# Four transposes of a head pair's outputs, spread between the products with V

## The chip, the cores and the metric

The kernel runs on one core of a Trainium2 chip. The metric is the device time of one execution in microseconds (us). Three runs of the kernel before gave 708.21, 708.3 and 709.0 us, so the median is 708.3 us.

## The reference

One transformer block with adaptive layer norm: 2048 tokens, model width 448, 16 heads of width 28, a sliding window of 256 keys, and a Mish feed-forward of width 1792.

```python
x = A_x
mod = (_silu(c) @ w_mod).reshape(c.shape[0], 6, 1, -1)
sa, ca, ga, sb, cb, gb = (mod[:, 0], mod[:, 1], mod[:, 2], mod[:, 3], mod[:, 4], mod[:, 5])
h = _layernorm(x, axis=-1) * (1 + ca) + sa
x = x + ga * _A_ref(h, A_wqkv, A_wo)       # softmax(mask(q k^T / sqrt(28))) v, then @ wo
h = _layernorm(x, axis=-1) * (1 + cb) + sb
x = x + gb * _B_ref(h, B_w1, B_b1, B_w2)   # mish(h @ w1 + b1) @ w2
```

All of it is float32. The mask keeps key k for query q where 0 <= q - k < 256.

## The kernel before

The 2048 tokens are cut into NG = 4 groups of GT = 512. For each group the kernel makes the normalized input, transposes it (`gen_hT`), and computes queries, keys and values (`gen_qkv`). Each float32 factor is split into a high and a low part, typed fp32r, and a product is made of the pairs high-high, high-low and low-high, so that one tile takes 11 matmuls.

Attention works on "slots". A slot i is one head of one group, and there are NS = 64 slots. Each slot has three units, so there are NU = 192 units u = 3i + b. A unit is one PSUM bank of scores: `B(u)` multiplies keys by queries (tile `sB`), adds the mask by bf16 products with an identity, and lets ScalarE write the exponentials twice (`P` in f32, `Ph` in fp32r). `SP(u)` lets GpSimd write the low part `Pl` = P - Ph. `PV(u, Ph)` and `PV(u, Pl)` multiply the two parts by V and add them up in the bank `pv` of the slot. V carries a column of ones, so that a row of `pv` is the softmax denominator. `A(i, t)` (tile `sA`) and `M2` find the row maxima that the scores are shifted by.

The units of a slot differ in shape. Unit b = 1 has two blocks of 256 columns in groups 1 to 3, and one block of 256 columns in group 0. The other two have blocks of 128 and 384 columns (group 0: one of 384, and both). A block is one matmul with V as its weights (60 columns).

When all three units of a slot are done, `EV(i)` copies `pv` into half of a tile `O2`: slots 2p and 2p+1 form head pair p (31 of the 32 pairs are touched by the change). `E(p)` transposes this tile by TensorE, in four steps of 128 tokens (124 rows, tile `et`, bank `tr`). `E2(p)` on ScalarE copies the low-part columns out (`ol`), and `E3(p)` on VectorE and GpSimd adds the parts, divides by the denominator and writes the result (`on`).

The order is written out by hand in one loop over u. Each engine runs its own instructions in program order. In step u = 3s + k the kernel writes, in this order: pending output steps, `PV(u-3, Pl)`, `EV`, `B(u)`, `SP(u-1)`, `A`, `M2`, loads, `E`/`E2`/`E3`, pieces of the next group's projections ("fillers"), a second `A`, and `PV(u-2, Ph)`. So the products of unit v with Ph end step v+2, and those with Pl begin step v+3: on TensorE they stand side by side. `E(p)` stands in step 6p+11, `E2(p)` in 6p+12 and `E3(p)` in 6p+13. The bank `tr` has one buffer, which `E` shares with `M2`.

Lines that the text speaks of: L679 `A`, L687 `M2`, L709 and L720 `B`, L723 and L724 its exponentials, L731 `SP`, L741 `PV`, L755 `E`, L760 `E2`, L768 to L771 `E3`, L250 transposes of a group's input (`tr`), L262 their low part (`hl`), L315 projection products, L595 an f32 product with a matrix of ones (`gb`), which is not split.

Of the kernel before, what the change touches and what calls it, by code (L numbers as in the profile page):

```python
# [14 lines left out]
S, D, F, H, DH, W = 2048, 448, 1792, 16, 28, 256  # L15
# [36 lines left out]
def adaln_block(ctx: ExitStack, tc: tile.TileContext, x, wqkv, wo, w1, b1, w2, c, w_mod, out):  # L52
    nc = tc.nc
    PE, ACT, DVE, POOL = nc.tensor, nc.scalar, nc.vector, nc.gpsimd
# [37 lines left out]
    def bank(tag, bufs, name):  # L92
        return PS[0].tile([128, 512], F32, name=name, tag=tag, bufs=bufs)
# [18 lines left out]
    for k in range(4):  # L112
        wmf = st0.tile([128, 2 * D], F32, name=f"wm01_{k}")
        t = wmf[0:112]
# [11 lines left out]
    for part in range(3):  # L126
        for ci in range(4):
            r0, r1 = ci * 128, min(ci * 128 + 128, D)
            for h in ((slice(0, 128),) if ci < 3 else (slice(0, 64), slice(64, 128))):
                t = wqs[ci][h]  # L130
# [9 lines left out]
    ident = cst.tile([128, 128], F32, name="ident")  # L140
# [164 lines left out]
    def drain(*gs):  # L305
        for g in gs:
            for _ in g:
                pipe.step()
# [17 lines left out]
    def flush():  # L326
        while later:
            later.pop(0)()
# [69 lines left out]
    for t in range(4):  # L398
        ln_stats(xs0[t][:, 0:D], mv0[:, t, :], qk, f"a0{t}")
        if t % 2:  # L400
            h = slice(t - 1, t + 1)
# [117 lines left out]
    O2 = []  # L519
    for i in range(2):  # L520
        t = att.tile([128, GT], F32, name=f"o2_{i}")
# [146 lines left out]
    NS = NG * H  # L668
    mx, Pt, Ph, Pl, pvb, et, olt = {}, {}, {}, {}, {}, {}, {}
    junk = att.tile([128, 384], F32, name="junk")  # L670

    def A(i, t):
        g, h = divmod(i, H)
        q, k = Q3[i % NQ], K3[i % NK]
        if i % 2 == 0 and t == 0:
            mx[i // 2] = att.tile([128, 2, 4], F32, name=f"mx{i}", tag="mx", bufs=2)
        c0 = max(256 - 128 * t, 0) if g == 0 else 0
        p = bank("sA", 2, f"sA{i}_{t}")
        PE.matmul(p[:, c0:384], q[0:84, t * 128:(t + 1) * 128], k[0:84, t * 128 + c0:t * 128 + 384],  # L679
                  start=True, stop=True)  # L680
        DVE.tensor_tensor_reduce(out=junk[:, c0:384], in0=p[:, c0:384], in1=mask[:, c0:384], scale=1.0,  # L681
                                 scalar=-3.0e38, op0=ALU.add, op1=ALU.max,
                                 accum_out=mx[i // 2][:, i % 2, t:t + 1])
# [11 lines left out]
    def units(g, b):  # L695
        return [x for x in BLOCKS[b] if g > 0 or x[0] >= 2]

    def by_width(blocks):
        return sorted(blocks, key=lambda x: x[2] - x[1])

    def B(u):
        i, b = divmod(u, 3)
        g, h = divmod(i, H)
        q, k = Q3[i % NQ], K3[i % NK]
        bl = units(g, b)
        c0 = bl[0][3]
        p = bank("sB", 2, f"sB{u}")
        for n, (jj, t0, t1, c) in enumerate(by_width(bl)[::-1]):
            PE.matmul(p[:, c:c + 128 * (t1 - t0)], k[:, jj * 128:(jj + 1) * 128], q[:, t0 * 128:t1 * 128],  # L709
                      start=(n == 0), stop=False, skip_group_check=True)  # L710
        far = {c + 128 * (jj - t0) for jj, t0, t1, c in bl if t0 <= jj < t1}
        diag = {c + 128 * (jj - 2 - t0) for jj, t0, t1, c in bl if t0 <= jj - 2 < t1}
        masked = []
        for c in sorted(far | diag):
            if c in far:
                masked.append((256 if c + 128 in diag else 128, c, 0))
            elif c - 128 not in far:
                masked.append((128, c, 128))
        for n, c, m in sorted(masked):
            PE.matmul(p[:, c:c + n], identr, fdmask[:, m:m + n], start=False, stop=True, skip_group_check=True)  # L720
        P = Pt[u] = att.tile([128, 512], F32, name=f"P{u}", tag="P", bufs=3)
        Ph[u] = att.tile([128, 512], F32R, name=f"Ph{u}", tag="Ph", bufs=3)
        ACT.activation(P[:, c0:], p[:, c0:], AF.Exp, scale=SCALE)  # L723
        ACT.activation(Ph[u][:, c0:], p[:, c0:], AF.Exp, scale=SCALE)  # L724

    def SP(u):
        i, b = divmod(u, 3)
        c0 = units(i // H, b)[0][3]
        Pl[u] = att.tile([128, 512], F32R, name=f"Pl{u}", tag="Pl", bufs=3)
        for eng, a, b in ((POOL, c0, 512),) if u < NU - 5 else ((POOL, 0, 256), (DVE, 256, 512)):  # L730
            eng.tensor_tensor(Pl[u][:, a:b], Pt[u][:, a:b], Ph[u][:, a:b].bitcast(F32), op=ALU.subtract)  # L731

    def PV(u, P):
        i, b = divmod(u, 3)
        g, h = divmod(i, H)
        if P is Ph and b == 0:
            pvb[i] = bank("sA", 2, f"pv{i}") if NS - 3 <= i < NS - 1 else bank("pv", 1, f"pv{i}")
        pv = pvb[i]
        for n, (jj, t0, t1, c) in enumerate(by_width(units(g, b))):
            j = 4 * g - 2 + jj  # L740
            PE.matmul(pv[0:60, t0 * 128:t1 * 128], V[j % NV][:, h, :], P[u][:, c:c + 128 * (t1 - t0)],  # L741
                      start=(P is Ph and b == 0 and n == 0), stop=False, skip_group_check=True)

    def EV(i):
        o = O2[i // 2 % 2][64 * (i % 2):64 * (i % 2) + 60]
        if i < NS - 3:
            ACT.activation(o, pvb[i][0:60, :], AF.Copy)  # L747
        else:
            DVE.tensor_copy(o, pvb[i][0:60, :])

    def E(pr):
        g, h = divmod(2 * pr, H)
        p = bank("tr", 1, f"et{pr}")
        for t in range(4):
            PE.transpose(p[:, t * 128:t * 128 + 124], O2[pr % 2][0:124, t * 128:(t + 1) * 128], ident[0:124, 0:124])  # L755
        et[pr] = p.rearrange("p (t a d) -> p t a d", t=4, a=2)

    def E2(pr):
        olt[pr] = att.tile([128, 4, 2, 28], F32, name=f"ol{pr}", tag="ol", bufs=2)
        ACT.activation(olt[pr], et[pr][:, :, :, 32:60], AF.Copy)  # L760

    def E3(pr):
        g, h = divmod(2 * pr, H)
        e, ol = et[pr], olt[pr]
        if h == 0:
            on[g] = mid.tile([128, 4, 512], F32, name=f"on{g}", tag="on")
        rc = att.tile([128, 4, 2, 1], F32, name=f"rc{pr}", tag="rc", bufs=2)
        DVE.reciprocal(rc, e[:, :, :, 28:29])  # L768
        DVE.tensor_tensor(ol, ol, e[:, :, :, 0:28], op=ALU.add)
        o = on[g][:, :, h * DH:(h + 2) * DH].rearrange("p t (a d) -> p t a d", a=2)  # L770
        POOL.tensor_tensor(o, ol, rc.to_broadcast([128, 4, 2, 28]), op=ALU.mult)  # L771
        if h == H - 2:
            POOL.tensor_copy(on[g][:, :, D:512], on[g][:, :, 384:448])
            on_full.add(g)
# [210 lines left out]
    def step(g):  # L985
        return next(fillers[g], 99.0) or RATE[g]
# [40 lines left out]
    for u in range(NU + 9):  # L1027
        s, k = divmod(u, 3)
        g = s // H
        if k == 0 and s % H == 0 and 0 < g < NG:  # L1030
            drain(fillers[g - 1], side[g - 1])
            flush()
        pipe.step()
        if 0 <= u - 3 < NU:
            PV(u - 3, Pl)
            if (u - 3) % 3 == 2:
                EV((u - 3) // 3)
        if u < NU:
            B(u)
        if 0 <= u - 1 < NU:  # L1040
            SP(u - 1)
        a = s + LEAD
        if a < NS:
            A(a, (0, 1, 3)[k])
        if k == 0 and (a - 1) % 2 == 1 and LEAD <= a - 1 < NS:
            M2((a - 1) // 2)
        if k == s % 2 and s < NS:
            load_slot(s + LEAD + 2)
        if s % 2 == 1 and 1 <= (s - 1) // 2 <= NS // 2:
            pr = (s - 3) // 2  # L1050
            if k == 2 and pr >= 0:
                E(pr)
        if s % 2 == 0 and k < 2 and 0 <= (s - 4) // 2 < NS // 2:
            (E2, E3)[k]((s - 4) // 2)
        if g < NG:
            v = u - 48 * g
            if v in (0, 12):
                chunk["v"] = 4 if v == 0 and g or 0 < g < NG - 1 else 2
            if v == 0:
                credit = 0.0  # L1060
            credit += RATE[g] * (2 if v < FRONT[g] else 1)
            while credit > 0.0:
                credit -= step(g)
            if v > 1 or g == 0:
                side_step(g, ("dve", "act")[a >= NS:] if k == 1 else ("act",) if k == 0 and s % 2 == 0 else ())
            if later and ((s + (k == 2)) % 2 == 0 or k == 1):
                later.pop(0)()
        if u == NU:
            drain(fillers[NG - 1], side[NG - 1])
            while pipe.items:  # L1070
                pipe.step()
            flush()
        if u - NU in TAIL:
            TAIL[u - NU]()
        if k == 1 and a < NS:
            A(a, 2)
        if 0 <= u - 2 < NU:
            PV(u - 2, Ph)
    for st in (FW["s2"], att_s, kq_s, vp_s):
        st.close()  # L1080
    psa_s.close()
# [68 lines left out]
    for n in range(NN + 1):  # L1150
        g, f = divmod(n, NF)
# [47 lines left out]
```

## Time and profile before

| | |
|---|---|
| median of three runs | 708.3 us |
| the profiled execution | 708.93 us, its span 707.1 us |
| TensorE busy (PE) | 687.4 us, 97% of the span |
| VectorE, ScalarE, GpSimd busy | 384.0, 391.4, 326.0 us |
| granted TensorE clock | 1.00 of full speed over the span |
| transposes of head pairs (L755) | 128, 268 ns each by the profile |

The profiled execution took 708.93 us, of which 1.8 us lie outside the span of its instructions. Durations below are from this execution. A matmul's duration in the profile covers its way through the array, and successive ones overlap; what a matmul costs the engine is the distance from its start to the next start.

### The profile page before, as it was taken

To read this page: it belongs to the slowest core of one execution; us is meant where nothing else is said; L and a number is where in the kernel's file an instruction comes from. 1 tells how busy PE (TensorE), PEld (TensorE's weight loads), DVE (VectorE), ACT (ScalarE), POOL (GpSimd) and SP (SyncE) were. 2 spreads that over 40 slices of the span, in tenths; PEclk is the share of its full clock that TensorE was granted. 3 is DMA by queue.
4 is the path that set the end of the run, shared out by engine and by line. 5 is a ranking of instruction groups with operands and counts; after the bars stand their busy time and mean duration, and the time that the engine had idled before them with its cause. 6 is when DMAs were issued, how large, how long until landed. Compare 5 with 4: busy or idle time off the path is not lost.

```text
span 707.1 us, 12019 instructions
## 1 busy us (share of the span) xinstructions
PE 687.4 (97%) x4001; PEld 589.0 (83%) x4001; DVE 384.0 (54%) x1030; ACT 391.4 (55%) x740; POOL 326.0 (46%) x355
## 2 busy tenths in 40 slices
PE   8899999999999999999999999999999999999997
PEld 8777888888898788898887788887888888888886
DVE  5688667688664888555767765452314222422112
ACT  3638778767766867767877974344223322332221
POOL 6626779586766677666778957313010000000000
PEclk9999999999999999999999999999999999999999
DMA  7865664454672462762774155810340035001001
GB/s 211 256 224 182 216 198 160 136 163 151 191 214 71 152 194 91 189 208 78 230 217 141 54 195 159 238 25 1 104 110 10 1 105 116 4 1 52 1 1 52
DMA packets 75177, 90.16 MB, mean 127 GB/s; under 512 B 31534, under 2 KB 51740, under 8 KB 75116
## 3 DMA queue, kind: packets, MB, share of 16 engines
q1 hardware_dynamic: 74652, 89.39, 42.1%
q8 instruction: 32, 0.52, 0.3%
q14 instruction: 29, 0.24, 0.1%
q10 hardware_dynamic: 464, 0.00, 0.0%
HBM read 56.60 MB, written 32.51 MB: 126 GB/s over the span
## 4 chain that ended last, share of the span: by engine, by line
PE 77%; DVE 9%; ACT 4%; issue 3%; POOL 1%; DMA 0%; DVEq 0%; ACTq 0%; POOLq 0%
PE z L913 19%; PE pv L741 9%; PE qk L315 8%; PE acc L1098 6%; PE acc L1096 6%; PE acc L1097 6%; PE sA L679 5%; PE sB L709 4%; PE wo L315 4%; PE qk_v L315 4%; PE sB L720 3%; DVE junk L681 3%; PE et L755 2%; ACT P L723 1%; ACT Ph L724 1%
## 5 line engine op out<-in xcount | busy, mean ns | idle before, releaser
L731 POOL TENSOR_TENSOR Pl<-P,Ph 128x512 fp32r<-128x512 f32 (+2 forms) x192 | 234.3, 1228 | 83.2 <-ACT Ph L724 44.7
L681 DVE CUSTOM_DVE_ANT_0 junk<-sA,mask 128x384 f32<-128x384 f32 (+2 forms) x256 | 135.2, 528 | 96.5 <-PE sA L679 88.3
L723 ACT ACTIVATE P<-sB 128x512 f32<-128x512 f32 (+2 forms) x192 | 109.8, 572 | 63.3 <-PE sB L720 58.3
L921 DVE TENSOR_TENSOR al<-t,ah 128x512 fp32r<-128x512 f32 x56 | 39.2, 700 | 181.8 <-ACT ah L920 181.8
L919 ACT ACTIVATE t<-z,b1c 128x512 f32<-128x512 f32 x56 | 38.3, 684 | 138.6 <-PE z L913 138.6
L724 ACT ACTIVATE Ph<-sB 128x512 fp32r<-128x512 f32 (+2 forms) x192 | 109.2, 569 | 0.0
L679 PE MATMUL sA<-k,q 84*128 84x384 f32 (+2 forms) x256 | 100.9, 396 | 2.3 <-DVE mx L681 1.5
L913 PE MATMUL z<-hlf,w 128*128 128x512 f32 x224 | 88.5, 395 | 0.0
L913 PE MATMUL z<-hhf,w 128*128 128x512 f32 x224 | 88.5, 395 | 0.0
L1096 PE MATMUL acc<-w2h,ah 128*128 128x448 f32 x224 | 82.2, 367 | 1.2 <-ACT ah L920 1.2
L1098 PE MATMUL acc<-w2h,al 128*128 128x448 f32 x224 | 82.0, 366 | 0.0
L1097 PE MATMUL acc<-w2l,ah 128*128 128x448 f32 x224 | 81.5, 364 | 0.0
L741 PE MATMUL pv<-Pl,v 128*60 128x256 f32 (+2 forms) x352 | 74.0, 284 | 3.8 <-POOL Pl L731 2.8
L741 PE MATMUL pv<-Ph,v 128*60 128x256 f32 (+2 forms) x352 | 76.6, 291 | 0.6 <-ACT o L747 0.5
L709 PE MATMUL sB<-q,k 86*128 86x256 f32 (+1 forms) x352 | 74.0, 284 | 0.2
L913 PE MATMUL z<-hhf,w1l 128*128 128x512 f32 x168 | 66.2, 394 | 0.0
L709 PEld LDWEIGHTS sB<-q,k 86*128 86x128 f32 x352 | 61.5, 189 | 1.8 <-issue 0.6
L720 PE MATMUL sB<-fdmask,identr 128*128 128x128 bf16 (+1 forms) x320 | 60.1, 253 | 0.0
L741 PEld LDWEIGHTS pv<-Ph,v 128*60 128x60 f32 x352 | 45.5, 133 | 14.6 <-ACT o L747 2.4
L679 PEld LDWEIGHTS sA<-k,q 84*128 84x128 f32 x256 | 48.9, 192 | 8.7 <-DVE mx L681 6.0
L741 PEld LDWEIGHTS pv<-Pl,v 128*60 128x60 f32 x352 | 45.0, 131 | 13.2 <-POOL Pl L731 5.4
L913 PEld LDWEIGHTS z<-hlf,w 128*128 128x128 f32 x224 | 42.1, 188 | 10.1
(159 smaller groups left out, 1249.8 us busy)
## 6 DMA issues: line engine op xcount, KB each, us to landing
scr<-st SPq DMA_DIRECT2D x24, 512.0 KB
k<-scr SPq DMA_DIRECT2D x48, 252.0 KB
q<-scr SPq DMA_DIRECT2D x64, 168.0 KB
scr<-st SPq DMA_DIRECT2D x32, 256.0 KB
x<-x1d SPq DMA_DIRECT2D x10, 448.0 KB
xin<-in_A_x_dram SPq DMA_DIRECT2D x8, 448.0 KB
xr<-in_A_x_dram SPq DMA_DIRECT2D x16, 224.0 KB
x1d<-xr SPq DMA_DIRECT2D x16, 224.0 KB
```

Of the source, the lines that this page charges most:

```text
L315: PE.matmul(p, b, a, start=(n == 0), stop=(n == 10))
L679: PE.matmul(p[:, c0:384], q[0:84, t * 128:(t + 1) * 128], k[0:84, t * 128 + c0:t * 128 + 384], start=True, stop=True)
L681: DVE.tensor_tensor_reduce(out=junk[:, c0:384], in0=p[:, c0:384], in1=mask[:, c0:384], scale=1.0, scalar=-3.0e38, op0=ALU.add, op1=ALU.max ...
L709: PE.matmul(p[:, c:c + 128 * (t1 - t0)], k[:, jj * 128:(jj + 1) * 128], q[:, t0 * 128:t1 * 128], start=(n == 0), stop=False, skip_group_ch ...
L723: ACT.activation(P[:, c0:], p[:, c0:], AF.Exp, scale=SCALE)
L724: ACT.activation(Ph[u][:, c0:], p[:, c0:], AF.Exp, scale=SCALE)
L731: eng.tensor_tensor(Pl[u][:, a:b], Pt[u][:, a:b], Ph[u][:, a:b].bitcast(F32), op=ALU.subtract)
L741: PE.matmul(pv[0:60, t0 * 128:t1 * 128], V[j % NV][:, h, :], P[u][:, c:c + 128 * (t1 - t0)], start=(P is Ph and b == 0 and n == 0), stop=F ...
L913: PE.matmul(zb[n], ps[m][1], ps[m][0], start=(m == 0), stop=(m == 10))
L1096: PE.matmul(p, ah[n][:, ts], w2h[f], start=(f == 0), stop=False)
L1097: PE.matmul(p, ah[n][:, ts], w2l[f], start=False, stop=False)
L1098: PE.matmul(p, al[n][:, ts], w2h[f], start=False, stop=(f == NF - 1))
```

## The change

`PV` takes a list of further calls ("ahead") and makes them between its matmuls. `E` now makes one transpose per call. For pairs 0 to 30 the first two transposes go into the products with Ph of unit 1 of slot 2p+3 (end of step 6p+12), the other two into the products with Pl of the same unit (begin of step 6p+13). `E2` follows them at once, and `E3` stays in step 6p+13. The last pair stays as it was.

```diff
-    def PV(u, P):
+    def PV(u, P, ahead=()):
...
-        for n, (jj, t0, t1, c) in enumerate(by_width(units(g, b))):
+        bl = by_width(units(g, b))
+        for n, (jj, t0, t1, c) in enumerate(bl):
             j = 4 * g - 2 + jj
+            for t in ahead[n * len(ahead) // len(bl):(n + 1) * len(ahead) // len(bl)]:
+                t()
             PE.matmul(pv[0:60, t0 * 128:t1 * 128], V[j % NV][:, h, :], P[u][:, c:c + 128 * (t1 - t0)],
...
-    def E(pr):
-        g, h = divmod(2 * pr, H)
-        p = bank("tr", 1, f"et{pr}")
-        for t in range(4):
-            PE.transpose(p[:, t * 128:t * 128 + 124], O2[pr % 2][0:124, t * 128:(t + 1) * 128], ident[0:124, 0:124])
-        et[pr] = p.rearrange("p (t a d) -> p t a d", t=4, a=2)
+    def E(pr, t):
+        if t == 0:
+            et[pr] = bank("tr", 1, f"et{pr}")
+        PE.transpose(et[pr][:, t * 128:t * 128 + 124], O2[pr % 2][0:124, t * 128:(t + 1) * 128], ident[0:124, 0:124])
+        if t == 3:
+            et[pr] = et[pr].rearrange("p (t a d) -> p t a d", t=4, a=2)
+
+    def turns(pr, t0):
+        return [lambda t=t: E(pr, t) for t in (t0, t0 + 1)] if 0 <= pr < NS // 2 - 1 else ()
...
+        pr = (s - 4) // 2 if s % 2 == 0 else -1
         if 0 <= u - 3 < NU:
-            PV(u - 3, Pl)
+            PV(u - 3, Pl, turns(pr, 2) if k == 1 else ())
+            if k == 1 and 0 <= pr < NS // 2 - 1:
+                E2(pr)
...
         if 0 <= u - 2 < NU:
-            PV(u - 2, Ph)
+            PV(u - 2, Ph, turns(pr, 0) if k == 0 else ())
```

On TensorE, at the old place of pair 18 (group 2), the kernel before has the four transposes between a product of `A` and the transposes of the next group's input; `tr` is that input's bank, `pv` the bank of slot 39:

```order
L720 MATMUL sB_4077<-fdmask,identr 128x256
L679 MATMUL sA_3_4088<-k_0_142,q_0_377 128x384
L755 MATMUL et_4091<-ident,o_0_463 128x124 x4
L250 MATMUL tr_4096<-ident,xin_2854 128x128 x4
L741 MATMUL pv_4101<-Ph_4017,v_171 60x128
L741 MATMUL pv_4101<-Ph_4017,v_173 60x384
```

In the changed kernel the same place on TensorE, with the same names (the numbers behind them differ), reads:

```order
L720 MATMUL sB_4077<-fdmask,identr 128x256
L679 MATMUL sA_3_4088<-k_0_142,q_0_377 128x384
L250 MATMUL tr_4091<-ident,xin_2854 128x128 x4
L744 MATMUL pv_4096<-Ph_4017,v_171 60x128
L744 MATMUL pv_4096<-Ph_4017,v_173 60x384
```

The four transposes are gone from this place, and the input's transposes follow the product of `A` at once. Their new place is unit 1 of slot 39 on TensorE, where `et` is the same bank `tr` and `v` are tiles of V:

```order
+L679 MATMUL sA_0_4115<-k_1_144,q_0_377 128x384
+L757 MATMUL et_4120<-ident,o_0_463 128x124
+L744 MATMUL pv_4096<-Ph_4051,v_172 60x256
+L757 MATMUL et_4120<-ident,o_0_463 128x124
+L744 MATMUL pv_4096<-Ph_4051,v_165 60x256
+L757 MATMUL et_4120<-ident,o_0_463 128x124
+L744 MATMUL pv_4096<-Pl_4086,v_172 60x256
+L757 MATMUL et_4120<-ident,o_0_463 128x124
+L744 MATMUL pv_4096<-Pl_4086,v_165 60x256
```

Each transpose now stands alone ahead of one 256-column product. In group 0, where unit 1 has one block, they stand two by two (pair 1, slot 5):

```order
L757 MATMUL et_1107<-ident,o_1_465 128x124 x2
L744 MATMUL pv_1084<-Ph_1042,v_167 60x256
L757 MATMUL et_1107<-ident,o_1_465 128x124 x2
L744 MATMUL pv_1084<-Pl_1073,v_167 60x256
L709 MATMUL sB_1117<-q_0_377,k_0_142 128x256
```

Seven pairs (0 to 6) have this form, 24 (7 to 30) the one before it. The order of VectorE, GpSimd and the DMA queue stays as it was. On ScalarE the copy `ol` moves behind one other instruction in five pairs and behind a table load in pair 30.

## Rows read from the trace of the kernel before

**Rows 1.** The page, busy time of each engine

```profile
PE 687.4 (97%) x4001; PEld 589.0 (83%) x4001; DVE 384.0 (54%) x1030; ACT 391.4 (55%) x740; POOL 326.0 (46%) x355
```

**Rows 2.** Windows of group 1 and attention's end: PE, PEld, DVE, ACT, POOL busy

```profile
120.00:220.00 100.00, 97.97 (x666) 85.02 (x665) 70.93 (x214) 71.49 (x139) 68.41 (x64) 1.00 0.53 161
380.00:420.00 40.00, 36.37 (x255) 29.89 (x254) 31.07 (x74) 33.60 (x65) 31.24 (x35) 1.00 0.35 113
```

**Rows 3.** Timeline of TensorE around one burst: start us, us, instruction

```profile
207.67 0.42 PE L679 MATMUL sA<-k,q 84*128 84x384 f32 x1
207.93 0.59 PE L755 MATMUL et<-ident,o 124*128 124x124 f32 x4
208.28 0.45 PE L315 MATMUL qk_v<-wql,hh 128*128 128x448 f32 x1
208.56 0.36 PE L315 MATMUL qk_v<-wq,hl 128*128 128x448 f32 x1
```

**Rows 4.** Timeline of TensorE, the same neighbours without transposes

```profile
205.61 0.42 PE L679 MATMUL sA<-k,q 84*128 84x384 f32 x1
205.87 0.37 PE L315 MATMUL qk_v<-wq,hh 128*128 128x448 f32 x1
206.08 0.37 PE L315 MATMUL qk_v<-wql,hh 128*128 128x448 f32 x1
```

**Rows 5.** Timeline of TensorE, 256-column products undisturbed

```profile
212.57 0.40 PE L741 MATMUL pv<-Ph,v 128*60 128x256 f32 x2
212.80 0.40 PE L741 MATMUL pv<-Pl,v 128*60 128x256 f32 x2
```

**Rows 6.** Timeline of TensorE, two f32 products of 448 columns

```profile
344.08 1.02 PE L595 MATMUL gb<-wm,ones 112*128 112x448 f32 x2
```

**Rows 7.** Timeline of weight loads behind them

```profile
344.56 0.13 PEld L741 LDWEIGHTS pv<-Ph,v 128*60 128x60 f32 x1 [0.19 <-issue]
344.94 0.14 PEld L741 LDWEIGHTS pv<-Ph,v 128*60 128x60 f32 x1 [0.24 <-issue]
```

**Rows 8.** Timeline of TensorE around one lone transpose (of row maxima)

```profile
217.05 0.42 PE L679 MATMUL sA<-k,q 84*128 84x384 f32 x1
217.31 0.27 PE L687 MATMUL mt<-ident,mx 128*8 128x128 f32 x1
...
217.62 0.36 PE L315 MATMUL qk_v<-wql,hh 128*128 128x448 f32 x1
```

**Rows 9.** Groups of weight loads by form: count | busy us, mean ns

```profile
L741 PEld LDWEIGHTS pv<-Ph,v 128*60 128x60 f32 x352 | 45.5, 133 | 14.6 <-ACT o L747 2.4 <-issue 0.6
...
L755 PEld LDWEIGHTS et<-ident,o 124*128 124x128 f32 x128 | 15.7, 140 | 0.8 <-ACT w L192 0.4
...
L687 PEld LDWEIGHTS mt<-ident,mx 128*8 128x8 f32 x32 | 2.7, 83 | 2.3 <-DVE mx L681 2.3
```

**Rows 10.** Timeline of TensorE, a lone transpose ahead of 256-column products

```profile
387.73 0.27 PE L687 MATMUL mt<-ident,mx 128*8 128x128 f32 x1
387.76 0.48 PE L741 MATMUL pv<-Ph,v 128*60 128x256 f32 x2
```

**Rows 11.** Waits of TensorE during attention: us, times, longest

```profile
PE tr L250 <- DVE hl L262: 1.6, 2, 0.8
```

**Rows 12.** Timeline of TensorE at pair 10

```profile
170.96 0.59 PE L755 MATMUL et<-ident,o 124*128 124x124 f32 x4
172.34 0.63 PE L250 MATMUL tr<-ident,xin 128*128 128x128 f32 x4 [0.79 <-DVE hl L262]
```

**Rows 13.** Windows, the stretch around pair 10 (columns as in rows 2)

```profile
170.00:177.00 7.00, 6.12 (x50) 5.28 (x49) 6.75 (x19) 6.40 (x14) 4.13 (x4) 1.00 0.52 159
```

**Rows 14.** Timeline of ScalarE at pair 9

```profile
162.58 0.36 ACT L760 ACTIVATE ol<-et 128x224 f32<-128x224 f32 x1
164.05 0.60 ACT L723 ACTIVATE P<-sB 128x512 f32<-128x512 f32 x1 [1.11 <-PE sB L720]
```

**Rows 15.** Timeline of TensorE at pair 9, products with Pl of unit 1

```profile
163.19 0.40 PE L741 MATMUL pv<-Pl,v 128*60 128x256 f32 x2
```

More of the change, by code (lines that the diff above doesn't have):

```diff
@@ L1048, in adaln_block @@
             load_slot(s + LEAD + 2)
[L1049 to L1054, printed above, removed]
+        if s == NS + 1 and k == 2:
+            for t in range(4):
+                E(NS // 2 - 1, t)
+        if pr == NS // 2 - 1 and k == 0:
+            E2(pr)
+        if pr >= 0 and k == 1:
+            E3(pr)
         if g < NG:
```

## The prediction, made before the result was known

> **What bounds the kernel now.** I read the page's busy times first. TensorE is busy 687.4 us of a span of 707.1 us, 97%, and no other engine passes 55% [rows 1]. Then the windows by stage: in group 1 of attention TensorE works 97.97 of 100 us, while VectorE, ScalarE and GpSimd stand near 70. Only in the last 40 us of attention does it fall to 36.37 of 40 us [rows 2]. The granted clock is 1.00 in both stretches, the level of 2.4 GHz. So between 50 and 380 us the end moves by what TensorE's queue becomes shorter or longer, and the question is what a transpose costs the engine at the old place and at the new one. As matmuls overlap in the profile, the cost is taken from start to start.
>
> **The change part by part: the transposes at the old place.** In the burst, the product of `A` starts at 207.67 us and the second projection product behind it at 208.56 us, 0.89 us later [rows 3]. The same three neighbours without transposes take 206.08 - 205.61 = 0.47 us [rows 4]. So a burst of four costs 0.42 us, 0.105 us for each. They are 31 bursts, 13 us in all. Nothing hides them.
>
> **What sets these 0.105 us.** A transpose has 124 moving columns. The products of V stream 256 columns in 0.23/2 = 0.115 us, 0.45 ns a column [rows 5]; at that rate a transpose would take 0.056 us. So there is room for two readings: either the f32 operand streams at half the rate, or a burst waits for the load of 128 weight columns before each transpose, and only the second can be hidden behind a longer product. Three rows speak for the first. The f32 product `gb` has 448 columns [rows 6]; a load of V begins when its second matmul begins, at 344.56, and the next load when the first product with V begins, at 344.94 [rows 7]. That is 0.38 us for 448 columns, 0.85 ns a column, with no load in the way; 124 columns at this rate are 0.105 us, the burst's own figure. Next, the transpose of the row maxima `mt` has only 8 weight columns and stands alone: from the product of `A` at 217.05 to the second projection product at 217.62 are 0.57 us [rows 8], 0.10 us more than the 0.47 us without it [rows 4]. A lone transpose with hardly a load thus costs as much as one in a burst. Last, its load is busy 83 ns, that of V (60 columns) 133 ns and that of the head pair's tile (128 columns) 140 ns [rows 9]; the last is hardly the longer one.
>
> The Trainium skill reads otherwise here. "TensorE: Matmul & The Clock Gate", section "LDWEIGHTS (loading the stationary operand)", puts a load at its columns divided by 1.2, in ns, whatever the rows, which for 128 columns is 107 ns. By that the burst would be bound by its loads, and behind a 256-column product each transpose would give some 0.05 us back; the sum would be that of the first rival. The trace disagrees as far as `mt` shows: 7 ns of load by the rule, and 0.10 us all the same.
>
> **The transposes at the new place.** The trace has no single transpose of 128 weight columns between products with V. The nearest row is `mt` ahead of two 256-column products: it starts at 387.73, the products 0.03 us later, and they last 0.48 us together [rows 10] against 0.40 us undisturbed [rows 5]. So it costs 0.03 + 0.08 = 0.11 us with 128 moving columns; the other row of a lone one says 0.10. From both sides: 0.10 to 0.11 us. I take 0.11, since there too V follows. Then 24 pairs (7 to 30) pay 4 x 0.11 = 0.44 us instead of 0.42, +0.02 us each, +0.5 us; with 0.10 it is -0.5 us. Seven pairs (0 to 6) stand two by two, 2 x (0.105 + 0.11) = 0.43 us, +0.07 us for the seven. The load of V behind a transpose is covered by the 0.105 us of that transpose, and the load of the transpose by the 0.115 us of the product before it; without that cover the second rival applies.
>
> **Waits at the old place.** A transpose that stands ahead of a wait for another engine is free, and moving it behind costs its full time. TensorE waits 1.6 us in attention, twice, for VectorE's `hl` before input transposes [rows 11]; one of these waits stands right behind the burst of pair 10: four transposes at 170.96, then 0.79 us idle until 172.34 [rows 12], and the other is the same place one group later, pair 18. Without the burst the wait ends as before, so 2 x 0.42 = 0.84 us can be lost. But VectorE is busy 6.75 of the 7 us around it [rows 13]: it is the bound there, and TensorE has to wait for it again anyway. The transposes come back inside the same stretch and fill such a wait. Between 0 and 0.84 us, I take 0.1.
>
> **ScalarE and what follows.** `E2` now waits for transposes of its own step and not for those of two steps earlier. At pair 9 ScalarE does `ol` at 162.58 for 0.36 us, and then sits 1.11 us until the next exponential at 164.05 [rows 14]. The products with Pl of that unit start at 163.19 and last 0.40 us [rows 15]. The last transpose goes before the second of them, some 0.1 us after 163.19, and its result should be there 0.27 us (its duration in the profile is that of `mt`, [rows 8]) later, at 163.57. `ol` then ends near 163.93, before 164.05. So this is free here, with about 0.1 us to spare; where it is late, the exponential is late by the same, and TensorE needs it only two steps on. VectorE's part of `E3` stands behind a product of `A` of the same step, which TensorE makes after the transposes. GpSimd's and the DMA queue's order is unchanged. The next `M2`, which shares the bank, comes two steps after `E3`, as before. I count nothing.
>
> **The sum.** +0.5 +0.07 +0.1 = about +0.6 us on TensorE, nothing elsewhere. Against the profiled execution's 708.93 us (span 707.1 and 1.8 outside it) that is 709.5 us; this execution lies 0.6 us over the median of the runs, so I put the forecast at 708.3 + 0.6 = 708.9 us.
>
> **The rivals.**
>
> First, loads hidden (faster). If bursts are bound by loads, a lone transpose costs 0.056 us at the rate of [rows 5]. Then 24 pairs save 4 x 0.05 = 0.20 us, 4.7 us, and seven pairs, where two of four are covered, 0.10 us each, 0.7 us: 702.9 us. For it: four equal steps of 0.105 us could be loads as well as streams, and no row has a full load behind a 256-column product. Against it: `mt` and `gb`. The page of the Trainium skill named above stands behind it.
>
> Second, a price for every change between transposes and products (slower). In the burst the product that follows takes 208.56 - 208.28 = 0.28 us [rows 3] against 206.08 - 205.87 = 0.21 us [rows 4]. I count these 0.07 us as the stream of the fourth transpose, whose successor is recorded as started only 0.03 us after it. If they are instead a cost of the change back to products, then a transpose itself takes 0.35/4 = 0.09 us, and four lone ones 4 x 0.16 = 0.63 us: +0.21 us on 24 pairs, +0.07 us on seven, 5.5 us: 713.8 us. It decides from the point where a transpose and its 256-column product take over 0.25 us together. Against it: lone `mt` costs 0.10 to 0.11, not 0.16.
>
> Third, waits (slower, small). The shade of both VectorE waits is lost (0.84 us) and the later `ol` delays exponentials where ScalarE is dense, in group 0 and the last 40 us; with some 0.1 us on ten pairs 708.9 + 0.8 + 1.0 = 710.7 us. For it: 6.75 of 7 us on VectorE. Against it: only two such places are in the list of waits, and exponentials are used two steps later.
>
> **How the numbers follow.** Forecast 70%, first rival 12%, second 8%, third 10%. The forecast's own range goes from -0.5 us (lone transposes at 0.10) to +1.4 us (0.11, and 0.84 us of waits), with half a microsecond of difference between runs 707.4 to 710.2. For 8 in 10 I reach to part of the outer cases, a third of the hidden loads (1.5 us) below and the third rival above: 706.8 to 711.0 us. A measurement of this kernel can tell about 0.2%, 1.4 us, from no change: the band is 706.9 to 709.7 us. Faster: the first rival and 2% of the forecast, 14%. Slower: the second, 6% of the third and 7% of the forecast, 21%. Within: 65%.
>
> **What would show it.** In the profile after, a transpose and the 256-column product behind it take 0.22 us from start to start if I am right, 0.17 if loads were the bound, 0.27 if each change costs. The unit that holds four takes 0.46 + 0.44 = 0.90 us from its first transpose to the next score product. TensorE's busy time stays at 687 us, and the places of pairs 10 and 18 show waits longer by up to 0.4 us. I am wrong if the unit takes 0.7 us or 1.1 us, or if TensorE's waits for ScalarE or GpSimd grow by a microsecond.

## The result, and the profile after

The changed kernel took 710.85 us (median of 14 runs, 709.38 to 712.48), the kernel before 709.25 us beside it (14 runs, 707.44 to 710.58): ratio 1.0026, 95% interval 1.0015 to 1.0037. So it is slower by 1.6 us. The forecast was +0.6 us and "no change" the likeliest; the time lies within the range, but the difference can be told from none. Of the 1.95 us between the forecast of 708.9 and the measured 710.85, 0.95 are the kernel before itself, whose three earlier runs had a median of 708.3. The profiled execution of after took 709.38 us (span 707.6), the lowest of its runs.

TensorE's busy time on the page, which answers to [rows 1], is what it was:

```profile
PE 687.7 (97%) x4001; PEld 590.0 (83%) x4001; DVE 386.0 (55%) x1030; ACT 394.2 (56%) x740; POOL 326.1 (46%) x355
```

The new place, on the timeline of TensorE after (start us, us, instruction), for pair 14; it answers to [rows 3, 5]:

```profile
224.97 0.27 PE L757 MATMUL et<-ident,o 124*128 124x124 f32 x1
225.00 0.37 PE L744 MATMUL pv<-Ph,v 128*60 128x256 f32 x1
225.20 0.27 PE L757 MATMUL et<-ident,o 124*128 124x124 f32 x1
225.23 0.36 PE L744 MATMUL pv<-Ph,v 128*60 128x256 f32 x1
225.43 0.27 PE L757 MATMUL et<-ident,o 124*128 124x124 f32 x1
225.46 0.37 PE L744 MATMUL pv<-Pl,v 128*60 128x256 f32 x1
225.66 0.27 PE L757 MATMUL et<-ident,o 124*128 124x124 f32 x1
225.69 0.36 PE L744 MATMUL pv<-Pl,v 128*60 128x256 f32 x1
225.89 0.40 PE L709 MATMUL sB<-q,k 86*128 86x256 f32 x2
```

A transpose and the product behind it take 0.23 us from start to start (224.97, 225.20, 225.43, 225.66, 225.89), so a lone transpose costs 0.23 - 0.115 = 0.11 us. The transposes therefore cost what they cost before, and the loss must be a wait. TensorE's list of waits in attention after (us, times, longest; first its matmuls, then its weight loads), which answers to [rows 9, 11]:

```profile
PE tr L250 <- DVE hl L262: 2.4, 2, 1.2
...
PE sB L709 <- DMA q<-mr: 0.7, 1, 0.7
```

```profile
PEld pv L744 <- ACT o L750: 5.2, 16, 0.6
```

VectorE's two waits grew from 1.6 to 2.4 us, as they should. New among the matmuls' is one of 0.7 us for the transfer of the row maxima. And the waits of V's load for ScalarE's copy `o`, which frees the bank `pv`, went from 2.4 us in 7 places [rows 9] to 5.2 us in 16.

To find the places I took the same score product of each head pair (the first of unit 6p+13, behind the new place) in both traces, and how much later after has it than before (TensorE's lag); the growth of the lag from pair to pair is what that pair cost. An ordinary pair costs between -0.02 and 0.06 us: -0.43 where the burst stood, +0.44 at the new place. Six do not: pairs 12, 14, 20, 22 and 27 cost 0.29 to 0.33 us each and pair 28 0.14, together 1.71 us. There the old place gave only about 0.10 us back. Pair 14 before, on TensorE, its loads and ScalarE:

```profile
221.52 0.59 ACT L747 ACTIVATE o<-pv 60x512 f32<-60x512 f32 x1
...
221.65 0.42 PE L679 MATMUL sA<-k,q 84*128 84x384 f32 x1
...
221.91 0.59 PE L755 MATMUL et<-ident,o 124*128 124x124 f32 x4
...
222.23 0.24 PEld L741 LDWEIGHTS pv<-Ph,v 128*60 128x60 f32 x2
```

and after:

```profile
221.38 0.59 ACT L750 ACTIVATE o<-pv 60x512 f32<-60x512 f32 x1
...
221.52 0.42 PE L679 MATMUL sA<-k,q 84*128 84x384 f32 x1
...
222.02 0.18 PEld L744 LDWEIGHTS pv<-Ph,v 128*60 128x60 f32 x2 [0.34 <-ACT o L750]
222.02 0.44 PE L744 MATMUL pv<-Ph,v 128*60 128x128 f32 x2
```

Before, the copy ends at 221.52 + 0.59 = 222.11, the burst fills TensorE until then, and V's load follows 0.12 us later without a wait. After, the copy ends at 221.97 and the load starts 0.05 us behind it: TensorE arrives 0.43 us earlier, waits 0.33 of it away, and then pays the transposes once more at the new place. The order has nothing between `A` and the first product of a slot at these pairs; at the others of groups 1 to 3 fillers or input transposes stand there, and before, the load came 0.36 to 1.9 us behind the copy.

Pairs 27 and 28 are a case of their own. What pair 27 costs comes back before the next old place: the lag is the same at 380.8 and at 387.1 us. At pair 28 a second wait stands behind the one for the copy, for VectorE's `x` (TensorE before, then after):

```profile
393.44 0.33 PE L250 MATMUL trf<-ident,x 128*128 128x128 f32 x1 [0.36 <-DVE x L241]
```

```profile
393.08 0.33 PE L250 MATMUL trf<-ident,x 128*128 128x128 f32 x1 [0.37 <-DVE x L241]
```

They lie 0.36 us apart, and the product of `A` ahead of the old place (390.72 and 390.37) 0.35. So taking the burst away brought nothing there, and pair 28 pays the whole 0.44 us of its new place; 0.14 us is that, less the 0.30 that pair 27 gets back.

The other places, of 0.64 us by which TensorE's lag grows over attention in this one pair of traces (-0.18 to +0.46): pairs 10 and 18 cost 0.48 and 0.44 and get 0.31 and 0.39 back in the next stretch, +0.22; the stretches behind pairs 7, 15 and 23 to 24 come 0.45, 0.41 and 0.50 us sooner, -1.36; pairs 4 and 6 +0.34 (at pair 6 it is the copy again: V's load came 0.27 us behind it before, and waits 0.21 us for it after); pair 29 and the scores behind it +0.36; and -0.73 at pairs 2 and 25, where the kernel before had two late transfers of row maxima in its profiled execution (the kernel "Three pairs that gain" below, in which both pairs stand as before and no such transfer is late, shows -0.37 and -0.39 there too). With 1.71 and 0.10 over all others this makes 0.64. Without the two late transfers it is 1.4 us, beside 1.6 us in the medians.

### The profile page after: what moved, and what is told of

Read it like the earlier page. It is cut to its first block, busy times and chain, and to the rows that moved or that the text cites. A ratio compares the mean times of both kernels' runs of the same rounds, so it can differ in the third digit from the quotient of the medians.

```text
span 707.6 us, 12048 instructions
## 1 busy us (share of the span) xinstructions
PE 687.7 (97%) x4001; PEld 590.0 (83%) x4001; DVE 386.0 (55%) x1030; ACT 394.2 (56%) x740; POOL 326.1 (46%) x355
## 4 chain that ended last, share of the span: by engine, by line
PE 74%; DVE 8%; ACT 4%; issue 3%; DMA 2%; POOL 2%; SPq 1%; DVEq 0%; POOLq 0%; ACTq 0%
PE z L919 16%; PE pv L744 10%; PE qk L315 8%; PE acc L1108 5%; PE sA L679 5%; PE acc L1106 5%; PE acc L1107 5%; PE sB L709 5%; PE qk_v L315 4%; PE sB L720 3%; PE wo L315 3%; DVE junk L681 2%; PE et L757 2%; POOL w1l L198 1%; SPq L59 1%
## 5 line engine op out<-in xcount | busy, mean ns | idle before, releaser
L744 PE MATMUL pv<-Ph,v 128*60 128x256 f32 (+2 forms) x352 | 81.3, 303 | 1.4 <-ACT o L750 0.6
L744 PE MATMUL pv<-Pl,v 128*60 128x256 f32 (+2 forms) x352 | 79.2, 296 | 2.8 <-POOL Pl L731 1.7
```

## The experiments

Three theories. S (shade): a burst that stands ahead of a wait fills time that would pass anyway, so what it costs hangs on the place. D: without the burst the row maxima's transfer has 0.43 us less time before the scores that need it. P: each single transpose costs more than one in a burst. Numbers by pair are the growth of TensorE's lag, as above.

**Eight pairs kept.** Pairs 10, 12, 14, 18, 20, 22, 27 and 28 as before, the other 23 as after.

```diff
-        return [lambda t=t: E(pr, t) for t in (t0, t0 + 1)] if 0 <= pr < NS // 2 - 1 else ()
+        return [lambda t=t: E(pr, t) for t in (t0, t0 + 1)] if moved(pr) else ()
...
+    def moved(pr):
+        return 0 <= pr < NS // 2 - 1 and pr not in {10, 12, 14, 18, 20, 22, 27, 28}
```

The rest of the edit leaves `E` and `E2` of a kept pair where the kernel before has them.

> Pairs 10, 12, 14, 18, 20, 22, 27 and 28 keep the burst of four at the old place; the other 23 pairs are as in the changed kernel. Theory S (the burst had stood in the shade of a wait: for ScalarE's copy that frees the bank of V's products in pairs 12, 14, 20, 22, 27, 28, and for VectorE in 10 and 18): the time goes back to that of the kernel before, ratio 0.9985 to 1.0005, and TensorE starts the first product of the new slot without a gap at those pairs. Theory D (the row maxima's transfer has 0.43 us less time before the scores that need it): most of the slowdown stays, ratio 1.0015 to 1.002. Theory P (every single transpose costs more than one in a burst): three quarters of it stay, ratio about 1.002.

Measured: 708.21 us, ratio 0.9985 (0.9975 to 0.9996). The kept pairs cost between -0.04 and +0.02 us. With 23 of 31 pairs still split, the kernel is faster than before: P falls, and so does D as the cause of the loss, since both expected most of it to stay.

**Only these eight** (the set turned round, `pr in {...}`).

> Only pairs 10, 12, 14, 18, 20, 22, 27 and 28 are changed; the other 23 keep the burst at the old place. S: six pairs open a gap of about 0.3 us before the first product of the new slot and lose it, 1.8 to 2.1 us in all, ratio 1.0025 to 1.003. D: a quarter of the slowdown, ratio about 1.0006. P: a quarter of it, ratio about 1.0006.

Measured: 710.77 us, 1.0019 (1.0009 to 1.0028), a little under what S expected, and above the 1.0006 of D and P. Pairs 12, 14, 20, 22 and 27 cost 0.31, 0.30, 0.30, 0.37 and 0.30 us, 28 0.14; 10 and 18 cost 0.46 and 0.42 and give 0.33 and 0.32 back. The waits of V's load for the copy are those of after:

```profile
PEld pv L744 <- ACT o L750: 4.8, 15, 0.6
```

By their ratios the two halves add up to 1.0004, and all 31 pairs are at 1.0026. The three intervals, some 0.7 us to either side each, cover this gap of 1.6 us only near their ends; it stays open.

**Four side by side at the new place**, in all 31 pairs.

```diff
-            PV(u - 3, Pl, turns(pr, 2) if k == 1 else ())
+            PV(u - 3, Pl)
...
-            PV(u - 2, Ph, turns(pr, 0) if k == 0 else ())
+            if k == 0:
+                for t in turns(pr, 0) and range(4):
+                    E(pr, t)
+            PV(u - 2, Ph)
```

> The four transposes stand side by side at the new place, ahead of the first 256-column product with Ph of unit 1, for all 31 pairs; nothing stands between products. S: the place decides, so the slowdown stays but for some 0.4 us, ratio 1.0015 to 1.0025. D: the same, since the transposes still stand behind the scores. P: without single transposes the slowdown is gone, ratio 1.000.

Measured: 710.0 us, 1.0007 (0.9997 to 1.0017): less than S and D expected, and P's 1.000 lies in the interval, so the ratio alone does not speak against P. The pairs do: the losses are those of after (0.29 to 0.42 at 12, 14, 20, 22), the gains too (-0.44 and -0.42 behind 7 and 15), and the new place costs 0.42 instead of 0.44 us, which is 0.5 us over 24 pairs. The medians of the two kernels lie further apart than that, with intervals that just touch; what of it is more than scatter stays open.

**Split at the old place.** The single transposes go between the products of unit 0, at the end of step 6p+11 and the begin of 6p+12, right behind where the burst stood.

```diff
+            PV(u - 3, Pl, turns(pr, 2) if k == 0 else ())
...
-            PV(u - 2, Ph, turns(pr, 0) if k == 0 else ())
+            PV(u - 2, Ph, turns((s - 3) // 2, 0) if s % 2 == 1 and k == 2 else ())
```

> The transposes stand one by one between the products of unit 0 of the same slot, at the old place: the first is ahead of the first product of the new slot, the last two ahead of the score products that need the row maxima. S: one of four stays in the shade of the wait (0.11 of about 0.3 us), so two thirds of the loss at six pairs (about 1.3 us) and 0.4 us for the single ones, ratio 1.002 to 1.0025. D: the transfer keeps its time, ratio 1.000 to 1.0005. P: all 31 pairs are split, so the whole slowdown, ratio 1.0025.

Measured: 711.09 us, 1.0027 (1.0017 to 1.0037). Ordinary pairs cost -0.02 to 0.05, pairs 12, 14, 20, 22 and 27 0.20 to 0.27, pairs 10 and 18 0.45 and 0.44, which is not given back, and the stretches behind 7, 15 and 23 gain nothing. One transpose still stands ahead of the product that waits, and three behind it: at pair 14 V's load waits 0.25 us for the copy instead of 0.34, and the pair costs 0.20 instead of 0.33, as S expected. About 1 us of the total no theory forecast: pairs 5 and 6 cost 0.21 and 0.79, and at pair 6 TensorE waits 0.55 us for VectorE's row maxima. The ratio alone also suits P; the pairs do not.

**The copy shared**, to make the wait shorter: after, with the copy of six slots halved between ScalarE and VectorE.

```diff
-        if i < NS - 3:
+        if i in (26, 30, 42, 46, 56, 58):
+            ACT.activation(o[:, 0:256], pvb[i][0:60, 0:256], AF.Copy)
+            DVE.tensor_copy(o[:, 256:512], pvb[i][0:60, 256:512])
+        elif i < NS - 3:
```

> As the changed kernel, but in six slots (26, 30, 42, 46, 56, 58) the copy of the bank pv is shared: ScalarE takes columns 0 to 255, VectorE 256 to 511, so that the bank comes free some 0.25 us earlier. They are the slots whose copy the burst of pairs 12, 14, 20, 22, 27 and 28 hid. Theory S (what a burst costs depends on the wait behind it; at these six pairs the copy of pv becomes a wait of TensorE): at each of the six, TensorE comes 0.2 to 0.25 us sooner than in the changed kernel, 1.2 to 1.5 us in all; from 1.0026 to 1.0005 to 1.001 of the kernel before. The waits for that copy, 16 in the changed kernel, go back to about 10. Theories D (transfer of the row maxima) and P (a price for each lone transpose): the copy of pv is on nobody's path, 1.0026 as the changed kernel.

Measured: 714.64 us, 1.0077 (1.0064 to 1.009). The edit did the opposite of what it was meant to do. Pair 14, ScalarE, TensorE and VectorE:

```profile
222.94 0.38 ACT L750 ACTIVATE o<-pv 60x256 f32<-60x256 f32 x1
...
223.08 0.42 PE L679 MATMUL sA<-k,q 84*128 84x384 f32 x1
...
223.35 0.42 DVE L751 COPY o<-pv 60x256 f32<-60x256 f32 x1 [0.31 <-ACT o L750]
...
223.82 0.19 PEld L744 LDWEIGHTS pv<-Ph,v 128*60 128x60 f32 x2 [0.58 <-DVE o L751]
```

The second half waits for the first, so the bank comes free later: load minus `sA` is 0.74 us, against 222.02 - 221.52 = 0.50 in after. TensorE pays all of these 0.24 us: pairs 12, 14, 20 and 22 cost 0.24, 0.24, 0.23 and 0.24 us more than in after. At pairs 27 and 28 VectorE was busy with other work and the wait was over a microsecond. So the copy does set TensorE's pace at these places; that a shorter one would give time back was not shown.

**The same shared copy in the kernel before.**

> The kernel before with the same six shared copies and nothing else. Theory S: the copy lies in the shade of the burst at these six places, so that TensorE gains at most the 0.1 us each that the list of waits shows there (0.13 us from the copy's end to the load), 0 to 0.6 us in all: 0.999 to 1.000. Rival C (a faster copy is worth its 0.25 us in any kernel, and the burst has nothing to do with it): 1.2 to 1.5 us, 0.998.

Measured: 710.26 us, 1.0016 (1.0008 to 1.0025). It is the control of the last one: the same later copy costs 0.10, 0.09, 0.08 and 0.13 us at pairs 12, 14, 20 and 22 where the burst stands ahead of it, and 0.24 where it doesn't. The difference, 0.11 to 0.15 us, is about the 0.12 us that the burst left between the copy's end and the load (222.11 to 222.23 above). Most of the total comes from pair 27, where VectorE was late (+1.42, and -0.73 behind it).

**Three pairs that gain.** Only 7, 15 and 23 as after.

> Only pairs 7, 15 and 23 as in the changed kernel, the other 29 as in the kernel before. Theory S: at these three TensorE waits for GpSimd or VectorE some microseconds behind the new place, so the transposes there are free, and the old place gives its 0.43 us back: 0.42 + 0.42 + 0.23 = 1.07 us less, 0.9985. If the gains that the traces showed behind these pairs came from other moved pairs, or by chance: 1.000.

Measured: 707.62 us, 0.9981 (0.9972 to 0.9989). Behind the three pairs TensorE comes 0.46, 0.46 and 0.32 us sooner, as in after (0.45, 0.41, 0.50, the last with pair 24 moved too). What gives the time back are waits ahead of which the transposes now stand. TensorE's waits in the stretch behind pair 7 (137 to 147 us), matmuls and loads, before:

```profile
PE pv L741 <- POOL Pl L731: 0.7, 2, 0.4
```

```profile
PEld sA L679 <- DVE mx L681: 0.5, 2, 0.3
```

and after:

```profile
PE pv L744 <- POOL Pl L731: 0.4, 1, 0.4
```

```profile
PEld sA L679 <- DVE mx L681: 0.3, 1, 0.3
```

One wait of each is gone. GpSimd and VectorE get their input 0.43 us sooner because the burst is out of the way, and TensorE does the transposes in the time in which it would have waited for them. That is S with the sign turned.

**The best by place.** Four side by side at the new place in 20 pairs; pairs 4, 6, 10, 12, 14, 18, 20, 22, 27, 28 and 29 as before.

> Four transposes side by side (not single) at the new place for 20 pairs; pairs 4, 6, 10, 12, 14, 18, 20, 22, 27, 28, 29, 30's neighbours apart, that is these eleven, as in the kernel before. It is meant as the best of what the drifts by pair show. Theory S: the eight kept pairs gave 0.9985; pair 29 (0.4 to 0.8 us by the late transfer of row maxima) and pairs 4 and 6 (0.1 and 0.2 us) come on top: 0.9972 to 0.998. If S is wrong about places and the kept pairs were a chance of that run: 1.000 to 1.0007, as with four side by side in all pairs.

Measured: 707.08 us, 0.9979 (0.997 to 0.9989), faster than both kernels, and within what S expected. It can't be told from the last one, which moves three pairs alone.

**Two moved, two stay** at the eight pairs, the rest as before.

```diff
+        if 0 <= po < NS // 2:
+            for t in range(2 if moved(po) else 4):
+                E(po, t)
...
-            PV(u - 2, Ph, turns(pr, 0) if k == 0 else ())
+            PV(u - 2, Ph)
```

> As the kernel before, but at pairs 10, 12, 14, 18, 20, 22, 27 and 28 two of the four transposes move: transposes 0 and 1 stay side by side at the old place, 2 and 3 go singly between the products with Pl. Theory S: at the shaded pairs 0.33 of the burst's 0.43 us is free (with all four gone TensorE gained 0.10 us). Two gone (0.21 us) lay open 0.10 us of exposed time and 0.11 us of shade, so the old place still gives 0.10 us, and the new one costs 2 x 0.11 = 0.22: +0.12 us at each of pairs 12, 14, 20, 22, 27. A rival L (every transpose at the old place hides a like part of the wait): half of 0.31, +0.155 us. At pairs 10 and 18: nothing gained at the old place, +0.22 at the new one, up to all of it given back within a few us. In all +0.5 to +0.8 us, ratio 1.0005 to 1.0012.

Measured: 709.48 us, 1.0006 (0.9993 to 1.0018).

**One moved, three stay** (`range(3 ...)`, and only transpose 3 at the new place).

> The same with only transpose 3 moved; 0 to 2 stay at the old place. Theory S: the one that is gone (0.105 us) was the exposed part (0.10 us), and costs 0.11 us at its new place: +0.01 us at each of pairs 12, 14, 20, 22, 27, no wait for the copy of pv there. Rival L: a quarter of 0.31, +0.08 us each, and a short wait. In all S 0.0 to +0.3 us, L +0.5 to +0.7 us; on the total hardly told apart (1.0000 against 1.0008), but by the drift of TensorE's starts from pair to pair.

Measured: 709.26 us, 1.0002 (0.9993 to 1.0012). Pair 14, ScalarE, TensorE and its loads:

```profile
221.46 0.59 ACT L750 ACTIVATE o<-pv 60x512 f32<-60x512 f32 x1
...
221.86 0.48 PE L757 MATMUL et<-ident,o 124*128 124x124 f32 x3
...
222.11 0.21 PEld L744 LDWEIGHTS pv<-Ph,v 128*60 128x60 f32 x2
```

The copy ends at 222.05, and the load follows the third transpose at 222.11: three fill the wait, and a fourth is too much by 0.10 us. The cost of a pair by the number of transposes moved away from it (only eight, two moved, one moved), in us:

| pair | 4 moved | 2 moved | 1 moved |
|---|---|---|---|
| 12 | 0.31 | 0.08 | -0.01 |
| 14 | 0.30 | 0.07 | 0.00 |
| 20 | 0.30 | 0.09 | 0.00 |
| 22 | 0.37 | 0.10 | 0.04 |
| 27 | 0.30 | 0.09 | 0.01 |
| S expected | (0.30) | 0.12 | 0.01 |
| L expected | (0.31) | 0.155 | 0.08 |

The figures in brackets are what both started from. The cost is not in proportion to what is moved; it starts where the wait is no longer filled. L falls at these five. At pair 28, where the whole burst was free, the cost is in proportion, from 387.1 us on: 0.44, 0.25 and 0.12 us. The waits for the copy are 7 again, as before, in both kernels: 2.3 us.

## Why the prediction was wrong

**The price of a transpose: right.** 0.23 us with its product (0.22 forecast), the unit with four 225.89 - 224.97 = 0.92 us (0.90 forecast), TensorE busy 687.7 us. The 0.02 us per pair are there.

**First rival, loads hidden: refuted.** It wanted 0.17 us, and 0.23 was measured. The rule of the Trainium skill behind it ("TensorE: Matmul & The Clock Gate", "LDWEIGHTS (loading the stationary operand)") does not bound these transposes, since a load that has a 256-column product of 0.115 us to hide behind gave nothing back. That the transpose streams for its 0.11 us, and does not wait for V's load behind it, is argued from `gb` [rows 6, 7]; no run tried it. **Second rival, a price for each change: refuted** by the same rows (0.27), and by the ordinary pairs, which cost nothing.

**Pairs 10 and 18: right in kind.** The wait behind pair 10 grew by 0.43 us, as the timeline of TensorE after shows against [rows 12]:

```profile
170.07 0.42 PE L679 MATMUL sA<-k,q 84*128 84x384 f32 x1
171.71 0.63 PE L250 MATMUL tr<-ident,xin 128*128 128x128 f32 x4 [1.22 <-DVE hl L262]
```

Of 0.92 us lost at the two, 0.70 came back within the next stretch: +0.22 against the 0.1 that I took.

**The step that failed: "Waits at the old place".** Its rule, that a transpose ahead of a wait is free, was right, and it is most of the loss. But I looked for such places in the list of waits, which holds only what was left over of a wait. Where the burst filled it wholly, no wait stood in the list, and V's load just followed the copy after 0.12 us. So I counted two places of eight, and left out the six of 1.71 us. "Nothing hides them", said of all 31 bursts, was wrong for these six: about 0.33 of the 0.42 us was hidden. The sign that I had named came true: the waits of V's load for ScalarE grew by 2.8 us. The third rival named lost shade too, but priced the two VectorE places and a late `ol`, and held that "only two such places are in the list" against itself: its 710.7 us, 2.4 over the kernel before, is near the time, which is 1.6 over it, by luck and by the wrong mechanism. The sign of the rest of the sum is the same omission: that transposes which come to stand ahead of waits for `Pl` and `mx` become free was not looked for at the new place either, and that is 1.36 us to the good.

**ScalarE: right at pair 9, wrong at pair 29.** `ol` at pair 9 starts at 162.86 and ends at 163.22, and the exponential behind it waits for its scores until 163.41 (timeline of ScalarE after, answers to [rows 14]):

```profile
162.86 0.36 ACT L766 ACTIVATE ol<-et 128x224 f32<-128x224 f32 x1 [1.24 <-PE et L757]
163.41 0.60 ACT L723 ACTIVATE P<-sB 128x512 f32<-128x512 f32 x1 [0.19 <-PE sB L720]
```

Pair 29 is one of those whose `ol` moved behind another instruction (timeline of ScalarE before, then after):

```profile
403.43 0.36 ACT L760 ACTIVATE ol<-et 128x224 f32<-128x224 f32 x1
403.67 0.79 ACT L257 ACTIVATE hhf<-trf,cols 128x512 fp32r<-128x512 f32 x1
```

```profile
403.61 0.78 ACT L257 ACTIVATE hhf<-trf,cols 128x512 fp32r<-128x512 f32 x1
404.27 0.36 ACT L766 ACTIVATE ol<-et 128x224 f32<-128x224 f32 x1
```

VectorE, which waits for `ol`, starts `E3` at 404.74 instead of 403.88, and TensorE then waits for VectorE's half of a `Pl` (before, then after):

```profile
407.57 0.33 PE L741 MATMUL pv<-Pl,v 128*60 128x256 f32 x1 [0.74 <-DVE Pl L731]
```

```profile
407.88 0.33 PE L744 MATMUL pv<-Pl,v 128*60 128x256 f32 x1 [0.94 <-DVE Pl L731]
```

From 405.6 to 408.6 us the lag grows by 0.25 to 0.36 us in the four kernels with this pair at the new place, and in none of the others. So "I count nothing" left out some 0.3 us here.

**"GpSimd and the DMA queue's order is unchanged ... I count nothing": wrong in one place.** The burst also stood between `M2` and the score product that needs the row maxima by DMA, so that the transfer has 0.43 us less. At pair 29 it came too late (TensorE after, start us, us):

```profile
400.80 0.40 PE L744 MATMUL pv<-Pl,v 128*60 128x128 f32 x2
401.89 0.47 PE L709 MATMUL sB<-q,k 86*128 86x384 f32 x2 [0.69 <-DMA q<-mr]
```

All four kernels with this pair at the new place wait there (0.33 to 0.81 us); none of the other eight, before among them, does. So D holds for this pair. It cost little: of the 0.88 us that after lags at 402.9 us, 0.11 are left at 405.3, since the next products wait for `Pl` either way.

## What to carry to other kernels

Work on a bound engine is free while it fills a wait, so moving it costs or gains by the waits at its old and its new place, and not by its own length. A wait that the work fills is missing in the list of waits: before moving something, take each of its places apart and see when the releasers of what stands behind it end; a next instruction that starts behind such an end by less than the work takes is a hidden wait. Here that was 0.12 us at the six pairs and 0.27 at pair 6, with work of 0.42 us. Move only the places that gain, as the two fastest kernels here do.

## What the runs showed of the hardware

A lone f32 transpose of 124 columns between products costs 0.11 us, as in a burst. Two engines' copies out of one bank, written as independent halves, ran one after the other here: VectorE's half began 0.03 us after ScalarE's ended, and the bank came free 0.24 us later than with one copy of 0.59 us. Whether the chip or the order of waits in the program makes it so was not tried. And the transfers of row maxima land late now and then in single executions, at pairs that an edit left alone (TensorE's matmuls wait 0.20 to 0.84 us for them at pairs 2 and 25 in "Only these eight" and "One moved, three stay"), which is as much as one of the effects looked for here.
